# Four raw buffers for the input weights, their loads a chunk ahead, and an earlier start for converting the output weights, in an attention kernel with two feed-forward layers

## Chip, cores and metric

The kernel runs on one core of a Trainium2 chip. The metric is the device time of one execution in microseconds (us). Instructions go to five engines, each with its own in-order queue: TensorE (PE, matrix products), VectorE (DVE), ScalarE (ACT), GpSimd (POOL) and SyncE (SP). SP and ACT also issue the DMA transfers. A matmul has a weight load (PEld) beside it.

## What is computed

The first part is attention in two steps, over 8 batches of 8 heads, 576 positions, head size 64, with 32 packed queries p per head. Then two feed-forward layers follow on 4608 tokens, with d_model 512 and d_ff 2048:

```python
p_packed = sm_attn(p, k, v)                  # softmax(p k^T / 8) v
out = sm_attn(q, p_packed, p_packed)
x = out.transpose(0, 2, 1, 3).reshape(B * S, H * D)
h = x @ w_in;   x = (h * cos(h)) @ w_out     # first layer
h = x @ w_in2                                # second layer
g = where(h >= 1, h, where(h <= -1, 0, (h + 1)**2 / 4));  return g @ w_out2
```

Inputs are 64-bit floats.

## The kernel before

Weights arrive as 64-bit floats. A tile of 128 x 512 of them is loaded as pairs of 32-bit words (512 KB), and `convert` (L126 to L142) turns it into 32-bit floats: one ACT pass over the high words (L132) and five DVE passes (L134, L135, L138, L139, L142). `split` (L66 to L68) then writes a value as a high and a low part, one ACT copy (L67) and one subtraction on DVE or POOL (L68), so that three matmuls (`TERMS`) make a product of full precision.

The work is written as Python generators, one queue ("stream") each for loads, weights, attention, and so on. The main loop takes one step of each stream per item. A scheduler then orders the instructions of each engine by a timeline of its own, so that neighbours in the program may change places. The order is fixed when the kernel is built.

The stages are these:

1. Opening. `cut_w_in(c)` (L397) loads and converts the input weights `w_in` in 4 chunks of 4 tiles. Only two buffers `raw` hold loaded words: two loads are issued ahead, and each further load is issued once a tile has been converted. Beside it run the attention of the first batches (`stage1`, `stage2`) and `form_first`, which forms M = p_packed times `w_in` (matmuls at L426, moves of the parts by DMA at L447, split into `m` tiles). The tile pool `mpool` has 6 buffers of 8 KB for `m`.
2. Batches. 128 items `up(n, hf, fp)` (L604) run over 8 batches n, two halves hf and 8 pairs fp. An item is 12 matmuls into `hps` (L618), a copy to `u` (on ACT at L627, on DVE at L625 for every fourth item) and a store of `u` to DRAM (`h1T<-u`, issued by ACT at L86). `hps` has two banks. In the stream "wo" runs `cut_w_out` (L509): 16 tiles of `w_out` are loaded (L518, by SP, into two buffers that attention used before), converted and split into `wo`. The `wo` tiles take the buffers of the pool `wpool` that held the input weights `wi`, after their last matmul. The M of later batches is loaded by SP as `ml<-mB` (L498).
3. First down product, `run_down1` (L779). Tiles `h` are loaded from DRAM (L776, SP), ACT scales them (L792), DVE removes the whole turns (L793), ACT takes the sine (L800, after one table load), DVE multiplies (L801), `split` makes `r` (L67, L68), and the matmuls at L827 take `r` and `wo`. The tiles `h`, `t` and `r` lie in memory that the tiles of stages 1 and 2 had, and wait until those are free. Beside it `combine` converts and combines the second layer's weights (tiles `raw`, `pa`, `pl`, stores `su<-raw` and `su<-pl`).
4. `run_up2` and `run_down2`, which the change does not touch.

The line that starts the conversion of `w_out` is in the loop over items:

```python
if n == B - 3 and fp == 0 and hf == 1:
    streams["wo"].append(cut_w_out())
```

In the changed kernel, lines behind L393 have numbers higher by 7 to 9: L407 loads `w_in` there, L526 loads `w_out`, L626, L633 and L635 are the items' matmul and copies, L801, L802, L809, L810 are ACT's scaling, DVE's turns, the sine and DVE's product of `run_down1`.

Of the kernel before, what the change touches and what calls it, by code (L numbers as in the profile page):

```python
# [11 lines left out]
I32 = mybir.dt.int32  # L12
# [15 lines left out]
def body(ctx: ExitStack, tc: tile.TileContext, q, k, v, p, w_in, w_out, w_in2, w_out2, out):  # L28
    nc = tc.nc
    B, HP, _, S = q.shape  # L30
# [9 lines left out]
    NCH = DFF // 512  # L40
# [6 lines left out]
    mpool = ctx.enter_context(tc.tile_pool(name="mpool", bufs=6))  # L47
# [18 lines left out]
    def split(hi, lo, src, eng=None):  # L66
        nc.scalar.activation(out=hi, in_=src, func=AF.Copy)  # L67
        (eng or nc.gpsimd).tensor_tensor(out=lo, in0=src, in1=hi.bitcast(F32), op=ALU.subtract)  # L68
        return hi, lo
# [4 lines left out]
    def behind(last):  # L74
        return tc.issue_after(last[-1]) if last else nullcontext()
# [44 lines left out]
    def drain(*names):  # L120
        while any([step(name)[0] for name in names or streams]):
            pass

    def words(src):
        return src.bitcast(I32)

    def convert(raw, a, after=()):

        hi, lo = raw[..., 1], raw[..., 0]
        hf, lf = raw.bitcast(F32)[..., 1], raw.bitcast(F32)[..., 0]  # L130
        with behind(after):
            nc.scalar.activation(out=hf, in_=hf, func=AF.Copy, scale=2.0 ** -112)  # L132
        ai = a.bitcast(I32)
        nc.vector.tensor_scalar(out=ai, in0=hi, scalar1=3, scalar2=None, op0=ALU.logical_shift_left)  # L134
        nc.vector.scalar_tensor_tensor(  # L135
            out=ai, in0=hi, scalar=-(1 << 31), in1=ai, op0=ALU.bitwise_and, op1=ALU.bitwise_or
        )
        nc.vector.tensor_scalar(out=hi, in0=ai, scalar1=-(1 << 23), scalar2=None, op0=ALU.bitwise_and)  # L138
        nc.vector.scalar_tensor_tensor(  # L139
            out=lf, in0=lo.bitcast(U32), scalar=2.0 ** -52, in1=hf, op0=ALU.mult, op1=ALU.mult  # L140
        )
        nc.vector.tensor_tensor(out=a, in0=a, in1=lf, op=ALU.add)  # L142
# [11 lines left out]
    stg = ph2.enter_context(tc.tile_pool(name="stg", bufs=1, side="right"))  # L154
# [180 lines left out]
    def stage2(m, bufs=bufs_b):  # L335
        yield from until(("pt", m))
        if m:
            yield from until(("at", m - 1, 1))
        ts = [load_T(q, m, G, bufs, "q" if late else "qk") for G in range(2)]
        xs = att.tile([128, 4, NTB, 32], F32, tag="x", name="x")  # L340
        yield

        def evac(G, hf, ps):
            nc.vector.transpose(out=xs[:, 2 * hf + G], in_=ps[:, :HB].rearrange("p (a b) -> p a b", b=32))

        yield from scores(ts, bufs, lambda hp: PT[m][:, hp], evac)
        ready.add(("s2", m))
        x = xs.rearrange("p i a b -> p (i a) b")
        mx = wk.tile([128, 4 * NTB], F32, tag="mx2", name="mx2")
        nc.vector.tensor_reduce(out=mx, in_=x, axis=AX.X, op=ALU.max)  # L350
        nc.gpsimd.tensor_tensor(
            out=x, in0=x, in1=mx.unsqueeze(2).to_broadcast([128, 4 * NTB, 32]), op=ALU.subtract
        )
        yield
        with tc.high_priority(offset=PRI_EXP):
            nc.scalar.activation(out=xs, in_=xs, func=AF.Exp, scale=scale)
        yield
        sm = wk.tile([128, 4 * NTB], F32, tag="sm2", name="sm2")
        nc.vector.tensor_reduce(out=sm, in_=x, axis=AX.X, op=ALU.add)
        nc.vector.tensor_scalar(out=sm, in0=sm, scalar1=1e-9, scalar2=None, op0=ALU.add)  # L360
        nc.vector.reciprocal(out=sm, in_=sm)
        yield
        for hf in range(2):
            i = slice(2 * NTB * hf, 2 * NTB * hf + 2 * NTB)
            nc.gpsimd.tensor_tensor(
                out=x[:, i], in0=x[:, i], in1=sm[:, i].unsqueeze(2).to_broadcast([128, 2 * NTB, 32]), op=ALU.mult
            )
            X[m, hf] = x[:, i]
        yield
        ready.add(("x", m))  # L370

    def weights_T(m, hf):
        yield from until(("x", m))
        if m == 1:
            at = stg.tile([128, 2, 2, HB], F32R, tag="at1", name="at1", bufs=2)
        else:
            at = wk.tile([128, 2, 2, HB], F32R, tag="at", name="at")
        a32 = wk.tile([128, 2, HB], F32, tag="y2", name="a32", bufs=1)
        nc.vector.transpose(out=a32.rearrange("p g (a b) -> p (g a) b", b=32), in_=X[m, hf])
        yield  # L380
        split(at[:, :, 0], at[:, :, 1], a32)
        AT[m, hf] = at
        yield
        ready.add(("at", m, hf))
# [8 lines left out]

    WI = {}

    def cut_w_in(c):
        def load(hp):  # L397
            raw = stg.tile([128, 512, 2], I32, tag="raw", name="raw", bufs=2)
            src = words(w_in[hp * 128:(hp + 1) * 128, c * 512:(c + 1) * 512])
            nc.sync.dma_start(out=raw, in_=src.rearrange("p (c t) -> p c t", t=2))  # L400
            return raw

        raws = [load(hp) for hp in range(2)]
        for hp in range(4):
            if hp % 2 == 0:
                t = wpool.tile([128, 2, 2, 512], F32R, tag="w", name="wi")
            a = stg.tile([128, 512], F32, tag="w32", name="w32", bufs=2)  # L407
            convert(raws[hp], a)
            yield
            if hp < 2:  # L410
                raws.append(load(hp + 2))
            split(t[:, hp % 2, 0], t[:, hp % 2, 1], a, nc.vector)
            WI[c, hp] = t[:, hp % 2]
            ready.add(("wi", c, hp))
            yield
# [92 lines left out]
    def make_M(n, c):  # L508
        streams["load"].append(load_M(n, c))  # L509
# [121 lines left out]
    def spare(pool, tag, name, n):  # L631
        return [pool.tile([128, 2048], F32, tag=tag, name=f"{name}{i}") for i in range(n)]

    kv = spare(wpool, "w", "kv", 4)
    nk, nv = 2 * S, (KC + 1) * 4 * D  # L635
    pp1 = wk.tile([128, 2, 2, HB], F32, tag="at", name="pp1").rearrange("p a b c -> p (a b c)")[:, :HP * 128]
    bufs_0 = Bufs([(ps_a, "psA"), (ps_a, "psC")])
# [135 lines left out]
    def load_h1(i):  # L773
        if i < B * 16:
            t = dn1["g"].tile([128, 2, HB], F32, tag="g", name="h1")
            nc.sync.dma_start(out=t, in_=h1T[i % 8, :, i // 8])  # L776
            G1[i] = t
# [215 lines left out]
    for i, (n, hf, fp) in enumerate(items):  # L993
        if i == n_first // 2:
            streams["mat"].append(stage2(2))
            make_M(2, 0)
            make_M(2, 1)
        if i in (n_first - 4, n_first - 2):
            streams["load"].append(weights_T(2, (i - n_first) // 2 + 2))
        if i == 3 * n_first // 4:  # L1000
            make_M(2, 2)
            make_M(2, 3)
        if i == n_first + 1:
            drain("wt")
            ph2.close()
            late.append(ph2.enter_context(
                tc.tile_pool(name="late", bufs=1, reuse_waits="tile", side="right")))
        if n == B - 3 and fp == 0 and hf == 1:
            streams["wo"].append(cut_w_out())
        if i >= n_first and fp == 0 and hf == 0 and n + 1 < B:  # L1010
            streams["mat"].append(stage2(n + 1))
            make_M(n + 1, 0)
            make_M(n + 1, 1)
        if n == B - 1 and hf and fp == 0:
            drain()
            ph2.close()
            ph1.close()
            for x in ("y", 0, 1, "d"):
                up2[x] = pu.enter_context(
                    tc.tile_pool(name=f"up_{x}", bufs=1, reuse_waits="tile", side="right"))  # L1020
            dn1["g"] = pd.enter_context(tc.tile_pool(name="dn_g", bufs=8, reuse_waits="tile", side="right"))
            dn1["r"] = pd.enter_context(tc.tile_pool(name="dn_r", bufs=4, reuse_waits="tile", side="right"))
            for j in range(7):
                load_h1(j)
        up(n, hf, fp)
        if i >= n_first:
            if fp == 7 and n + 1 < B:
                streams["load"].append(weights_T(n + 1, hf))
            if hf and fp in (1, 3) and n + 1 < B:
                make_M(n + 1, fp // 2 + 2)  # L1030
        begin_stores(1)
        for name in ("load", "wt", "wo", "frm", "mat", "att", "load", "mat", "att", *(("att",) if i < n_first else ())):
            step(name)
# [54 lines left out]
```

## Time and profile before

| | us |
|---|---|
| three runs: median (lowest to highest) | 1709.02 (1708.21 to 1716.55) |
| the profiled execution | 1708.01 |
| its span, first to last instruction | 1706.0 |
| PE busy | 1566.5 |
| DVE busy | 1228.0 |
| ACT busy | 938.1 |

The profile is of one execution. Its own time lies 2.0 us above its span. The mean clock that TensorE was granted is 0.953 of its full 2.4 GHz; at its lower level of 1.2 GHz a stretch shows 0.50. A stage is best read by a table of windows: how long each engine was busy in a stretch of the span, and the clock in it.

### The profile page before, as it was taken

How to read it: one execution, taken by the hardware profiler on the slowest of the kernel's cores; microseconds unless marked ns; L12 is line 12 of the kernel's file. 1: busy time of each engine (PE TensorE's matmuls, PEld its weight loads, DVE VectorE, ACT ScalarE, POOL GpSimd, SP SyncE). 2: the span in 40 equal slices, each digit the busy share in tenths (PEclk: the TensorE clock that was granted, in tenths of full speed). 3: DMA queues.
4: the chain of work that ended last, by engine and by line, in shares of the span. 5: the costliest groups of instructions: out<-in, count | busy, mean ns of one | idle time of the engine just before them, and what ended most of it. 6: DMA issues, size and time to landing. Idle time of an engine off the chain costs nothing.

```text
span 1706.0 us, 28414 instructions
## 1 busy us (share of the span) xinstructions
PE 1566.5 (92%) x10846; PEld 1504.0 (88%) x10846; DVE 1228.0 (72%) x1787; ACT 938.1 (55%) x1530; POOL 231.9 (14%) x154
## 2 busy tenths in 40 slices
PE   9579988999819999999999989989999799999998
PEld 7459876998809999999998988889999799999998
DVE  6873434457869889987773889979766687777774
ACT  4443443445447667776663666766766444444443
POOL 1220101221100200000003224434331000000000
PEclk7779998999959999999999999999999899999999
DMA  7666797797667677664337455654437844444431
GB/s 258 161 194 215 226 298 242 234 298 255 239 200 220 194 268 245 212 204 131 113 91 272 153 184 207 212 208 167 174 133 308 339 151 131 128 132 139 139 105 36
DMA packets 177993, 333.23 MB, mean 195 GB/s; under 512 B 16576, under 2 KB 70848, under 8 KB 174272
## 3 DMA queue, kind: packets, MB, share of 16 engines
q1 hardware_dynamic: 123584, 237.02, 44.5%
q10 hardware_dynamic: 54272, 94.39, 14.8%
q8 instruction: 85, 1.39, 0.3%
q14 instruction: 52, 0.43, 0.1%
HBM read 190.84 MB, written 136.31 MB: 192 GB/s over the span
## 4 chain that ended last, share of the span: by engine, by line
PE 60%; DMA 16%; DVE 16%; issue 4%; ACT 3%; SPq 1%; ACTq 0%; DVEq 0%
PE psZ L932 9%; PE hps L618 8%; PE psZ L827 7%; PE psY L932 6%; PE psX L932 5%; PE psZ L747 5%; PE psX L747 3%; DMA raw<-in_moe_w_out 3%; PE psX L827 3%; PE psY L827 3%; PE psY L747 3%; DMA raw<-in_moe_w_in 3%; PE psA L279 2%; DVE t L733 2%; DVE raw L139 1%
## 5 line engine op out<-in xcount | busy, mean ns | idle before, releaser
L67 ACT ACTIVATE r<-g 128x576 fp32r<-128x576 f32 x224 | 153.4, 686 | 180.2 <-PE psZ L932 71.6
L618 PE MATMUL hps<-at,m 128*128 128x288 f32 x1536 | 234.8, 307 | 16.7 <-ACT u L627 8.2
L618 PEld LDWEIGHTS hps<-at,m 128*128 128x128 f32 x1536 | 216.4, 193 | 28.8 <-ACT u L627 10.7
L68 DVE TENSOR_TENSOR r<-g,r 128x576 fp32r<-128x576 f32 x224 | 166.7, 755 | 70.2 <-ACT r L67 70.1
L827 PE MATMUL psZ<-r,wo 128*128 128x288 f32 x1536 | 206.6, 296 | 0.9 <-DVE r L68 0.9
L827 PEld LDWEIGHTS psZ<-r,wo 128*128 128x128 f32 x1536 | 205.3, 188 | 1.4 <-DVE r L68 1.4
L827 PE MATMUL psX<-r,wo 128*128 128x288 f32 x768 | 125.9, 298 | 38.7 <-ACT r L67 35.8
L932 PE MATMUL psZ<-r,sw 128*128 128x288 f32 x1152 | 158.2, 296 | 1.6 <-DVE o L725 0.9
L932 PEld LDWEIGHTS psZ<-r,sw 128*128 128x128 f32 x1152 | 155.0, 188 | 2.0 <-issue 1.1
L827 PEld LDWEIGHTS psX<-r,wo 128*128 128x128 f32 x768 | 110.6, 190 | 40.2 <-ACT r L67 36.0
L733 DVE SCALAR_TENSOR_TENSOR t<-hh,t 128x576 f32<-128x576 f32 x128 | 119.0, 937 | 34.5 <-ACT t L732 33.3
L731 ACT ACTIVATE t<-hh,half 128x576 f32<-128x576 f32 x128 | 97.8, 771 | 61.5 <-DVE hh L725 45.3
L68 DVE TENSOR_TENSOR r<-t,r 128x576 fp32r<-128x576 f32 x128 | 99.3, 776 | 39.5 <-ACT r L67 39.4
L747 PE MATMUL psZ<-ty,sw 128*128 128x288 f32 x768 | 114.5, 299 | 14.2 <-DVE hh L725 14.2
L68 POOL TENSOR_TENSOR ty<-td,ty 128x576 fp32r<-128x576 f32 x32 | 55.1, 1726 | 522.6 <-DMA yT<-o 320.4
L827 PE MATMUL psY<-r,wo 128*128 128x288 f32 x768 | 124.1, 297 | 0.0
L747 PEld LDWEIGHTS psZ<-ty,sw 128*128 128x128 f32 x768 | 106.1, 190 | 16.8 <-DVE hh L725 16.8
L67 ACT ACTIVATE r<-t 128x576 fp32r<-128x576 f32 x128 | 87.1, 680 | 51.5 <-PE psY L827 26.7
L932 PE MATMUL psX<-r,sm 128*128 128x288 f32 x768 | 107.5, 300 | 8.5 <-ACT r L67 8.3
L932 PEld LDWEIGHTS psX<-r,sm 128*128 128x128 f32 x768 | 105.3, 192 | 9.1 <-ACT r L67 8.6
L827 PEld LDWEIGHTS psY<-r,wo 128*128 128x128 f32 x768 | 110.2, 189 | 0.0
L800 ACT ACTIVATE t<-t,halfpi 128x576 f32<-128x576 f32 x128 | 97.9, 768 | 19.9 <-DVE t L793 19.7
(164 smaller groups left out, 2833.6 us busy)
## 6 DMA issues: line engine op xcount, KB each, us to landing
h1T<-u ACTq DMA_DIRECT2D x128, 288.0 KB, 3.3
h<-h1T SPq DMA_DIRECT2D x128, 288.0 KB, 3.4
gT<-t ACTq DMA_DIRECT2D x128, 288.0 KB, 2.7
g<-gT SPq DMA_DIRECT2D x128, 288.0 KB, 3.2
raw<-in_moe_w_in SPq DMA_DIRECT2D x32, 512.0 KB, 5.6
raw<-in_moe_w_out SPq DMA_DIRECT2D x32, 512.0 KB, 4.9
mB<-cp SPq DMA_DIRECT2D x96, 128.0 KB, 3.6
ml<-mB SPq DMA_DIRECT2D x48, 256.0 KB, 4.5
```

Of the source, the lines that this page charges most:

```text
L67: nc.scalar.activation(out=hi, in_=src, func=AF.Copy)
L68: (eng or nc.gpsimd).tensor_tensor(out=lo, in0=src, in1=hi.bitcast(F32), op=ALU.subtract)
L139: nc.vector.scalar_tensor_tensor(out=lf, in0=lo.bitcast(U32), scalar=2.0 ** -52, in1=hf, op0=ALU.mult, op1=ALU.mult)
L279: nc.tensor.matmul(out=pp[:, s * 64:s * 64 + 64], lhsT=ve[:, s * 128:s * 128 + 128], rhs=e[:, pos * 64:pos * 64 + 64], start=(c == 0), sto ...
L618: nc.tensor.matmul(out=hps[:, j, :HB], lhsT=m[:, w, G, cs], rhs=x[:, G, y], start=(G == 0 and i == 0), stop=(G == 1 and i == 2),)
L731: nc.scalar.activation(out=t, in_=h, func=AF.Relu, scale=0.5, bias=half)
L733: nc.vector.scalar_tensor_tensor(out=t, in0=h, scalar=1.0, in1=t, op0=ALU.max, op1=ALU.min)
L747: nc.tensor.matmul(out=ps[:, i], lhsT=s[:, d, w, cs], rhs=t[:, d, y], start=first and d == n == 0, stop=d == 1 and n == 2, skip_group_chec ...
L800: nc.scalar.activation(out=t, in_=t, func=AF.Sin, scale=2 * PI, bias=halfpi)
L827: mm = nc.tensor.matmul(out=acc[d // 2][:, d % 2], lhsT=wo[f // 4, w][:, f % 4, ds], rhs=r[:, y, k], start=f == n == 0, stop=f == NFT - 1 ...
L932: nc.tensor.matmul(out=ps[:, j], lhsT=s[:, f % 4, w, j * 128:j * 128 + 128], rhs=r[:, y, k], start=first and f == n == 0, stop=f == 7 and ...
```

## The change

The opening gets four buffers for loaded words instead of two. The third and fourth (`raw2`) are made from one 8 KB tile of `mpool`, which M uses later. All four tiles of chunk 0 are loaded at the start, and each conversion of chunk c is followed at once by the load of the same tile of chunk c + 1. And `cut_w_out` is put into its stream one batch (16 items) sooner.

```diff
     def cut_w_in(c):
-        def load(hp):
-            raw = stg.tile([128, 512, 2], I32, tag="raw", name="raw", bufs=2)
+        def load(c, hp):
+            i = n_raw[0] % 4
+            n_raw[0] += 1
+            if i < 2:
+                raw = stg.tile([128, 512, 2], I32, tag="raw", name="raw", bufs=2)
+            else:
+                raw = raw2[:, i - 2].rearrange("p (c t) -> p c t", t=2)
...
-        raws = [load(hp) for hp in range(2)]
+        if c == 0:
+            ahead[0] = [load(0, hp) for hp in range(4)]
         for hp in range(4):
...
-            convert(raws[hp], a)
+            convert(ahead[c][hp], a)
+            if c + 1 < NCH:
+                ahead.setdefault(c + 1, []).append(load(c + 1, hp))
             yield
-            if hp < 2:
-                raws.append(load(hp + 2))
             split(t[:, hp % 2, 0], t[:, hp % 2, 1], a, nc.vector)
...
+    raw2 = spare(mpool, "m", "raw", 1)[0].bitcast(I32).rearrange("p (a b) -> p a b", b=1024)
...
-        if n == B - 3 and fp == 0 and hf == 1:
+        if n == B - 4 and fp == 0 and hf == 1:
             streams["wo"].append(cut_w_out())
```

On SP, at the start of the program, the queue before issues two loads of `w_in` words and then the values v of attention:

```order
L400 DMA raw<-in_moe_w_in 128x1024 x2
L221 DMA vraw<-in_v 128x4x256
L224 DMA vraw<-in_v 64x256
L221 DMA kv_122<-in_v 128x4x256
L224 DMA kv_122<-in_v 64x256
L195 DMA qk<-in_q 128x2x576 x2
L309 DMA pp<-in_p 128x512
L400 DMA raw<-in_moe_w_in 128x1024
```

The same place in the changed kernel (`raw_124` is the tile `raw2`):

```order
L407 DMA raw<-in_moe_w_in 128x1024 x2
L407 DMA raw_124<-in_moe_w_in 128x1024 x2
L221 DMA vraw<-in_v 128x4x256
L224 DMA vraw<-in_v 64x256
L221 DMA kv_122<-in_v 128x4x256
L224 DMA kv_122<-in_v 64x256
L195 DMA qk<-in_q 128x2x576 x2
L309 DMA pp<-in_p 128x512
L407 DMA raw<-in_moe_w_in 128x1024
```

Two loads have moved ahead of all loads of v and q.

On DVE, at the end of the items, the queue before starts with the last copy of an item (L625) and goes on with the conversion of `w_out` (the tiles `w_4187`, `w_4230` and `w_4273` are three of its last four; the last one and a piece of `combine` follow):

```order
L625 COPY u<-hps 128x576
L134 TENSOR_SCALAR w_4230<-raw 128x512
L68 TENSOR_TENSOR wo<-w_4187,wo 128x512
L135 SCALAR_TENSOR_TENSOR w_4230<-raw,w_4230 128x512
L138 TENSOR_SCALAR raw<-w_4230 128x512
L139 SCALAR_TENSOR_TENSOR raw<-raw 128x512
L134 TENSOR_SCALAR w_4273<-raw 128x512
L142 TENSOR_TENSOR w_4230<-w_4230,raw 128x512
L135 SCALAR_TENSOR_TENSOR w_4273<-raw,w_4273 128x512
L138 TENSOR_SCALAR raw<-w_4273 128x512
L68 TENSOR_TENSOR wo<-w_4230,wo 128x512
```

In the changed kernel DVE's queue has, up to and behind the last copy of an item (L633; `w_4023` is the last tile of `w_out`):

```order
L68 TENSOR_TENSOR wo<-w_3968,wo 128x512
L138 TENSOR_SCALAR raw<-w_4023 128x512
L633 COPY u<-hps 128x576
L139 SCALAR_TENSOR_TENSOR raw<-raw 128x512
L142 TENSOR_TENSOR w_4023<-w_4023,raw 128x512
L68 TENSOR_TENSOR wo<-w_4023,wo 128x512
L633 COPY u<-hps 128x576
L802 SCALAR_TENSOR_TENSOR t<-h_4354,t 128x576
L802 SCALAR_TENSOR_TENSOR t<-h_4356,t 128x576
```

Four of the 16 splits into `wo` stand behind the last copy before, and none after. Counted in items on DVE and ACT, the splits stand at items 92 to 128 before and at 77 to 125 after.

On ACT, at the start of `run_down1`, the queue before ends the last `wo` and the first unit of `combine` before it begins (the names in brackets are what a row waits for: DMAHW0 to DMAHW7 are DMA transfers):

```order
L67 ACTIVATE wo<-w_4316 128x512 [waits DVE_49]
L67 ACTIVATE raw<-raw 128x512 [waits DMAHW2_49,DMAHW3_49,DVE_49,Activation_49]
L67 ACTIVATE pl<-raw 128x512 [waits DMAHW4_49,DVE_49,Activation_49]
L792 ACTIVATE t<-h_4361 128x576 [waits DMAHW5_49,Pool_49]
L792 ACTIVATE t<-h_4363 128x576 [waits DMAHW6_49]
L800 ACT_TABLE_LOAD
```

In the changed kernel it begins with the last stores of the items:

```order
L635 ACTIVATE u<-hps 128x576 [waits DMAHW3_49,DMAHW0_49,PE_49]
L86 DMA h1T<-u 128x576 [waits Activation_49]
L86 DMA h1T<-u 128x576 [waits DMAHW4_49,DVE_49]
L801 ACTIVATE t<-h_4354 128x576 [waits DMAHW6_49,Pool_49]
L801 ACTIVATE t<-h_4356 128x576 [waits DMAHW7_49,DMAHW4_49,DMAHW0_49]
L801 ACTIVATE t<-h_4358 128x576 [waits DMAHW1_49]
L801 ACTIVATE t<-h_4360 128x576 [waits DMAHW2_49]
L809 ACT_TABLE_LOAD
L809 ACTIVATE t<-t,halfpi 128x576 [waits DVE_49] x4
L67 ACTIVATE r_4525<-t 128x576 [waits DVE_49]
```

The piece of `combine` has moved behind the first `r`, and the second scaling waits for two more transfers than before.

## Rows read from the trace of the kernel before

**Rows 1.** The page: busy time of each engine, share of the span, instructions.

```profile
PE 1566.5 (92%) x10846; PEld 1504.0 (88%) x10846; DVE 1228.0 (72%) x1787; ACT 938.1 (55%) x1530; POOL 231.9 (14%) x154
```

**Rows 2.** Windows: stretch, its length, busy time and instructions by engine, clock, DMA.

```profile
12.00:118.30 106.30, 74.93 (x280) 55.63 (x279) 92.01 (x166) 49.90 (x104) 22.30 (x13) 0.70 0.67 193
20.00:40.00 20.00, 19.38 (x73) 16.15 (x74) 15.12 (x33) 8.84 (x26) 2.14 (x2) 0.50 0.61 190
363.00:395.00 32.00, 31.98 (x228) 30.91 (x227) 18.29 (x25) 15.88 (x26) 9.11 (x6) 1.00 0.78 276
395.00:474.80 79.80, 67.93 (x475) 63.94 (x473) 67.45 (x110) 41.95 (x70) 9.44 (x6) 1.00 0.74 248
474.80:510.60 35.80, 0.05 (x1) 0.05 (x1) 23.68 (x39) 13.49 (x21) 0.00 (x0) 0.53 0.59 193
510.60:770.00 259.40, 255.61 (x1891) 253.89 (x1892) 233.72 (x346) 185.11 (x291) 8.74 (x5) 0.99 0.69 224
```

**Rows 3.** Timeline around the stretch 474.8 to 510.6: start, us, engine, line, operation, tiles, count.

```profile
471.12 3.63 PE L618 MATMUL hps<-at,m 128*128 128x288 f32 x24 [2.17 <-ACT u L627]
...
498.35 0.68 DVE L68 TENSOR_TENSOR wo<-w,wo 128x512 fp32r<-128x512 f32 x1
...
499.63 4.51 SPq L776 DMA_DIRECT2D h<-h1T  x8
...
506.05 1.28 ACT L800 ACT_TABLE_LOAD   x1
...
510.55 0.61 PE L827 MATMUL psX<-r,wo 128*128 128x288 f32 x1 [35.80 <-ACT r L67]
```

**Rows 4.** Tile t, 495 to 530 us: ns min/median/max, first and last start.

```profile
L792 ACT ACTIVATE t<-h x12: 667/668/687, 504.6 to 528.0; 128x576 int32<-128x576 f32 x12
...
L800 ACT ACTIVATE t<-t,halfpi x11: 759/763/777, 507.3 to 529.7; 128x576 f32<-128x576 f32 x11
...
L67 ACT ACTIVATE r<-t x9: 668/672/692, 509.8 to 529.1; 128x576 fp32r<-128x576 f32 x9
```

**Rows 5.** The page, DMA issues: count, KB each, median us to landing.

```profile
h1T<-u ACTq DMA_DIRECT2D x128, 288.0 KB, 3.3
```

**Rows 6.** DVE by line, 363 to 475 us: busy, mean ns, idle before.

```profile
L625 DVE COPY u<-hps 128x576 f32<-128x576 f32 x15 | 11.3, 752 | 8.5 <-PE hps L618 6.8 <-DMA h1T<-u 1.3 <-issue 0.4
```

**Rows 7.** Waits of DVE, 12 to 126 us.

```profile
DVE w L134 <- ACT raw L132: 9.6, 8, 1.9
```

**Rows 8.** Tile raw, 0 to 130 us: first ACT pass, and time from issue to landing.

```profile
L132 ACT ACTIVATE raw<-raw x16: 651/676/698, 11.8 to 106.4; 128x512 f32<-128x512 f32 x16
...
DMA to landing us min/median/max: 3.8/5.1/8.7
```

**Rows 9.** Timeline of the opening: first load and first use of v.

```profile
4.89 0.44 SPq L221 DMA_DIRECT2D vraw<-in_v  x1
...
15.57 1.00 PE L279 MATMUL psA<-e,vraw 128*128 128x64 f32 x8
```

**Rows 10.** Windows of the opening, and tile vraw: time from issue to landing.

```profile
6.00:8.00 2.00, 2.00 (x10) 1.58 (x9) 0.00 (x0) 0.47 (x2) 0.00 (x0) 1.00 1.05 407
...
DMA to landing us min/median/max: 4.4/5.7/9.9
```

**Rows 11.** PE by line, 395 to 474.8 us.

```profile
L618 PE MATMUL hps<-at,m 128*128 128x288 f32 x463 | 66.0, 300 | 11.8 <-ACT u L627 7.4 <-DVE u L625 4.3
```

**Rows 12.** Tile wo, 280 to 520 us: the ACT half of its splits.

```profile
L67 ACT ACTIVATE wo<-w x16: 612/630/636, 401.4 to 496.8; 128x512 fp32r<-128x512 f32 x16
```

**Rows 13.** Timelines of DVE and of POOL, 415.5 to 420 us.

```profile
416.61 2.62 DVE L68 TENSOR_TENSOR wo<-w,wo 128x512 fp32r<-128x512 f32 x1
...
416.24 2.45 POOL L351 TENSOR_TENSOR x<-x,mx 128x1152 f32<-128x1152 f32 x1 [5.56 <-DVE mx L350]
```

**Rows 14.** Waits of SP's queue, 395 to 474.8 us.

```profile
SPq L518 <- DVE w L142: 41.4, 11, 8.1
```

**Rows 15.** Windows of tile pa (the first unit of combine) alone.

```profile
474.80:510.60 35.80, 6.26 (x10) 0.94 (x2) 0.53 0.59 193
```

More of the change, by code (lines that the diff above doesn't have):

```diff
@@ L394, in body @@
     WI = {}
+    n_raw, ahead = [0], {}
     def cut_w_in(c):
-        def load(hp):
-            raw = stg.tile([128, 512, 2], I32, tag="raw", name="raw", bufs=2)
+        def load(c, hp):
[5 more added lines that the diff above has]
+                raw = raw2[:, i - 2].rearrange("p (c t) -> p c t", t=2)
             src = words(w_in[hp * 128:(hp + 1) * 128, c * 512:(c + 1) * 512])
```

## The prediction

> **What bounds the kernel now.** I read the page first: PE is busy 92% of the span and no other engine comes near [rows 1]. So time is to be had only where PE stands still or runs at its lower clock, and the next view is a table of windows by stage [rows 2]. It shows two places that the edits touch. In the opening, 12 to 118.3 us, PE is busy for 74.9 of 106.3 us at a clock of 0.70, and DVE for 92.0: DVE sets the pace there. From 474.8 to 510.6 us PE has one matmul in 35.8 us. Ahead of that gap, among the last items, it loses some 12 of 79.8 us; behind 510.6 it is full, 255.6 of 259.4 us.
>
> The timeline around that gap comes next, with what ended each wait [rows 3]. The first matmul of the down product waits 35.8 us for ACT's first `r`, and the rows ahead say why. The last item's matmuls end at 471.12 + 3.63 = 474.75. The last piece of `wo` leaves DVE at 498.35 + 0.68 = 499.0. At 499.63 SP begins the loads of `h`, whose memory was in use until then, and at 510.55 PE starts. So 24.9 us of the gap pass until the loads, and 10.9 us are the restart proper. The 16 pieces of `wo` come at a pace of (496.8 - 401.4) / 15 = 6.4 us [rows 12]; the first comes too late for the last to be ready with the items' end.
>
> **The gap.** The change starts the conversion a batch sooner. On DVE no split into `wo` stands behind the last copy of an item any more. I therefore take the 24.9 us out and work out a new restart from the order on ACT: the last copy of an item, 0.75 [rows 6]; its store, which the second scaling waits for (its memory was that of a `u`), 3.3 to landing [rows 5]; three more scalings at 0.67 (2.0), the table load 1.28 [rows 3], four sines at 0.76 (3.05) and the first copy into `r`, 0.67 [rows 4]. That is 11.05 us, so the gap shrinks by 35.8 - 11.05 = 24.8. If the wait is for an older store, the 4.05 fall to one copy and one scaling more, 0.75 + 0.67: the gap is 8.4 and the gain 27.4. If `wo` ends late and `h` is loaded only after the last copy, the 10.9 of today's restart come behind a rest of one tile, 6.4 by its pace: 17.3, and a gain of 18.5. The order speaks for the middle value.
>
> The Trainium skill (ScalarE: Activation LUTs, What ACT_TABLE_LOAD costs) adds a drain to a table switch and gives some 2.66 us in all. The row shows 1.28. By the page the new gap would be 1.4 us longer.
>
> What the gap covered has to run elsewhere: the first unit of `combine`, 6.26 us of DVE on its tile `pa` alone [rows 15]. It moves under the first down product, where DVE is idle for 259.4 - 233.7 = 25.7 us up to 770 [rows 2]. Hidden it costs 0; without cover 6.3 and some smaller passes, 9 at most (estimate: half as much again). I take 1.5, nearer to hidden, since DVE at 90% sometimes delays an `r`.
>
> **The batches.** The conversion itself is not less work. The order has the splits at items 77 to 125, so about 15 items earlier; at 32.0 us / 228 = 0.14 us a matmul [rows 2] and 12 an item that is 25 us, to a start near 376 and, at 6.4 us a piece, an end near 472, just ahead of the last item. From 395 to 474.8 PE now loses 11.8 us to late copies of `u` on ACT and DVE [rows 11], queued behind conversion work. Two things change: about four more tiles fall among the items (4 / 12 of 11.8 is 4 us more), and they are spread, (125 - 77) / 15 = 3.2 items a tile where the order before had (128 - 92) / 15 = 2.4, so that copies wait less (a quarter, 3 us less). I take 0, with bounds of -8 (most of the wait goes) and +8 (twice that for the four more tiles).
>
> Moved forward, the tiles also meet more work of POOL: 9.1 us of it in the 32 from 363 to 395, against 9.4 in the 79.8 behind [rows 2]. The trace shows what that does: one subtraction of DVE takes 2.62 us beside a POOL pass of 2.45, where the next to the gap takes 0.68 [rows 13, 3]. Prorated, 9.1 - 9.4 x 32 / 79.8 = 5.3 us of DVE time more. If it all delays the last `wo`, it eats 5.3 of the 24.8.
>
> The Trainium skill (SBUF — State Buffer, Who interferes with whom) says that a DVE instruction with two SBUF inputs and a GpSimd one that reads SBUF block each other fully, the later waiting for the earlier's end. It speaks against this change, which puts DVE's passes beside more of POOL's; the trace agrees in the pair above.
>
> **The opening.** DVE's work stays: 16 tiles by five passes and a split. What goes are waits: 9.6 us in 8 of them in which DVE waits for ACT's first pass [rows 7], which itself comes when a load has landed, 5.1 us after its issue in the median, 8.7 at most [rows 8]. The 16 first passes stand at 11.8 to 106.4 us, so 6.3 apart [rows 8]. With a load issued when its buffer's conversion ends and three tiles converted in between, a load has about 19 us for its 8.7: covered. I take 9 of the 9.6. The most is DVE's whole idle time, 106.3 - 92.0 = 14.3 [rows 2]; the least is 0, if SP's queue, in which the loads wait for their buffers, holds back the moves of M instead and DVE then waits for those.
>
> Against it stands that two loads more, 1.05 MB, go ahead of v and q. At 407 GB/s [rows 10] they delay these by 2.6 us. v is issued at 4.89 and used at 15.57 [rows 9], and lands 5.7 later in the median, 9.9 at most [rows 10]: 4.89 + 5.7 + 2.6 = 13.2 is in time, with 9.9 it is 17.4, 1.8 late. I take 0 and keep 1.8. M's buffers: one fewer while `raw2` lives, but the first M is used up four items in, and its buffer then serves; cost 0, and if it isn't, one or two items, 1.7 to 3.4.
>
> **Sum.** -9 (opening) - 24.8 (gap) + 1.5 (`combine`) + 0 (batches) = -32.3. The profiled execution took 1708.0 us (span 1706.0), 0.06% below the median of the runs shown. 1708.0 - 32.3 = 1675.7; I predict 1676.
>
> **The rivals.**
> - The opening gives nothing: DVE's idle time moves from waits on words to waits on M's parts, which SP queues behind the loads of words. For it: from 20 to 40 us PE is busy for 19.4 of 20 us at the lower clock [rows 2], so there a faster conversion feeds nobody. Against: the 8 waits are in DVE's own queue. 1708.0 - 24.8 + 1.5 + 1.8 = 1686.5.
> - The gap is not emptied: the tiles keep their pace or slow down by POOL's 5.3 us, and `wo` ends behind the last copy. For it: 472 is close to 474.8. Then the gap gains 18.5, and the batches lose up to 8: 1708.0 - 9 - 18.5 + 1.5 + 8 = 1690.
> - Slower: SP's queue. Loads of words wait there for DVE, 41.4 us in 11 waits, 8.1 at most [rows 14], and in the changed order ten of the 16 have loads of M for the last two batches behind them. M is asked for a batch ahead, 16 items or 27 us, which absorbs as much. At the mean, 3.8, ten waits are 38: 11 us late, still faster by 21. It decides from (27 + 32) / 10 = 5.9 us a wait; at 8.1 the end is 1708.0 - 32 + 81 - 27 = 1730. Against it: the waits can overlap with M's lead more than once.
> - The change doesn't do what it says: the starting batch moves nothing, because `wo` needs buffers of `wi`. Against: in the order the splits have moved by 15 items. About 1700 (opening only).
>
> **How the numbers follow.** Forecast: 0.68, by itself 1663 to 1688 (opening 14 to 4, gap 27.4 to 20, batches -5 to +2). Opening without gain: 0.13. Gap not emptied: 0.11. No effect of the start: 0.04. Slower: 0.02. Better than the forecast's range: 0.02. The range 1661 to 1692 leaves out the last three and a rest of the others, some 12 in 100. A measurement can tell about 0.5%, or 8.5 us, from no change. Faster by more: the first three and the best, 0.94, less a rest: 0.93. Within 0.5%: 0.05, slower: 0.02.
>
> **What the profile after would show.** Right: DVE waits for ACT's first pass of `w_in` words nearly gone, last input tile converted near 109 us instead of 118; the gap ahead of the first L836 matmul 8 to 13 us and behind it no `wo` left; PE's idle time among the items near 12 us; DVE nearer to full from 470 to 700. Wrong: a gap above 17 us, waits of the items' matmuls for `m` in the last batches, or a stretch to the end of the opening that is as long as before, with DVE or PE waiting for L455's moves.

## The result, and the profile after

The changed kernel takes 1679.91 us (median of 4 runs, 1676.02 to 1687.23) against 1709.67 for the kernel before on the same chip: a ratio of 0.985, 95% interval 0.982 to 0.987. On a second chip it was 1681.03 us (6 runs) against 1706.11, ratio 0.9856 [0.9833, 0.988]. The change is 25 to 30 us faster; 1676 was forecast, in a range of 1661 to 1692.

The profiled execution is the slowest of the first four (1687.23 us, span 1685.2), so its parts sum to 20.8 us and not to 30. Its page (busy time of each engine, to be set beside [rows 1]):

```profile
PE 1566.7 (93%) x10846; PEld 1506.5 (89%) x10846; DVE 1225.1 (73%) x1787; ACT 937.1 (56%) x1530; POOL 229.1 (14%) x154
```

The windows of the kernel after, columns as in [rows 2]; the third row is the new gap:

```profile
12.00:118.30 106.30, 74.46 (x293) 56.29 (x292) 93.14 (x166) 52.07 (x109) 19.47 (x14) 0.70 0.68 198
20.00:40.00 20.00, 19.30 (x98) 16.55 (x98) 18.95 (x40) 11.82 (x33) 3.19 (x4) 0.74 0.86 273
472.70:485.10 12.40, 0.08 (x2) 0.04 (x1) 6.24 (x9) 7.24 (x11) 0.00 (x0) 0.59 0.91 309
485.10:770.00 284.90, 277.87 (x2040) 276.37 (x2041) 252.12 (x375) 198.97 (x312) 8.82 (x5) 0.98 0.68 217
```

The gap is 12.4 us where it was 35.8. In the opening DVE is not less busy over the whole stretch, but in 20 to 40 us it is busy for 18.95 us instead of 15.12, and PE's granted clock there is 0.74 instead of 0.50. The down product, in contrast, is less full than it was: 7.0 us idle in 284.9, against 3.8 in 259.4.

The timeline around the new gap answers to [rows 3]:

```profile
469.73 0.69 DVE L68 TENSOR_TENSOR wo<-w,wo 128x512 fp32r<-128x512 f32 x1 [1.22 <-ACT wo L67]
473.03 0.76 DVE L633 COPY u<-hps 128x576 f32<-128x576 f32 x1 [2.61 <-DMA h1T<-u]
474.25 0.68 ACT L801 ACTIVATE t<-h 128x576 int32<-128x576 f32 x1 [2.41 <-DVE u L633]
478.52 1.83 ACT L801 ACTIVATE t<-h 128x576 int32<-128x576 f32 x3 [3.58 <-DMA h1T<-u]
480.36 1.28 ACT L809 ACT_TABLE_LOAD   x1
481.66 2.77 ACT L809 ACTIVATE t<-t,halfpi 128x576 f32<-128x576 f32 x4
484.34 1.24 ACT L67 ACTIVATE r<-t 128x576 fp32r<-128x576 f32 x2
485.06 0.61 PE L836 MATMUL psX<-r,wo 128*128 128x288 f32 x1 [12.32 <-ACT r L67]
```

The last split into `wo` ends at 470.4, ahead of the items' last matmul. What is left is the restart on ACT that the prediction added up: the last copy, the wait for a store of `u` (ACT stands idle for 3.58 us), three scalings, the table load, four sines, the first `r`. Tile `wo`, to be set beside [rows 12]:

```profile
L67 ACT ACTIVATE wo<-w x16: 615/628/641, 369.9 to 469.1; 128x512 fp32r<-128x512 f32 x16
```

The waits of PE from 465 to 900 us (what waited for what: us in total, times, longest) have the gap, and behind it 6.2 us for DVE's splits into `r`:

```profile
PE psX L836 <- ACT r L67: 12.3, 1, 12.3
PE psX L836 <- DVE r L68: 3.1, 2, 2.6
PE psZ L836 <- DVE r L68: 3.1, 2, 1.7
```

DVE's waits in the opening, to be set beside [rows 7]: the 9.6 us for ACT's first pass have become 1.0, and a wait for a product of `form_first` has grown from 7.0 (first row, of the kernel before) to 9.8.

```profile
DVE cp L430 <- PE psD L426: 7.0, 2, 6.6
```

```profile
DVE cp L438 <- PE psD L434: 9.8, 2, 7.9
DVE w L134 <- ACT raw L132: 1.0, 1, 1.0
```

### The profile page after: what moved, and what is told of

The parts are those of the page before. It is cut to its first block, busy times and chain, and to the rows that moved or that the text cites. A ratio compares the mean times of both kernels' runs of the same rounds, so it can differ in the third digit from the quotient of the medians.

```text
span 1685.2 us, 28435 instructions
## 1 busy us (share of the span) xinstructions
PE 1566.7 (93%) x10846; PEld 1506.5 (89%) x10846; DVE 1225.1 (73%) x1787; ACT 937.1 (56%) x1530; POOL 229.1 (14%) x154
## 4 chain that ended last, share of the span: by engine, by line
PE 52%; DVE 22%; DMA 17%; issue 5%; ACT 3%; SPq 1%; ACTq 0%; DVEq 0%
PE psZ L941 9%; PE hps L626 7%; PE psY L941 6%; PE psZ L836 5%; PE psX L941 5%; PE psZ L756 4%; DMA raw<-in_moe_w_in 3%; PE psY L756 3%; PE psX L756 2%; PE psY L836 2%; PE psX L836 2%; DVE t L742 2%; DVE r L68 2%; DVE t L802 2%; DVE raw L139 2%
## 5 line engine op out<-in xcount | busy, mean ns | idle before, releaser
L626 PE MATMUL hps<-at,m 128*128 128x288 f32 x1536 | 239.6, 311 | 16.7 <-ACT u L635 7.5
L626 PEld LDWEIGHTS hps<-at,m 128*128 128x128 f32 x1536 | 221.7, 197 | 28.9 <-ACT u L635 10.3
L836 PE MATMUL psX<-r,wo 128*128 128x288 f32 x768 | 126.0, 299 | 15.5 <-ACT r L67 12.3
L756 PE MATMUL psZ<-ty,sw 128*128 128x288 f32 x768 | 115.2, 300 | 15.0 <-DVE hh L734 15.0
L836 PEld LDWEIGHTS psX<-r,wo 128*128 128x128 f32 x768 | 111.2, 190 | 16.6 <-ACT r L67 12.6
```

The source lines that it names most:

```text
L626: nc.tensor.matmul(out=hps[:, j, :HB], lhsT=m[:, w, G, cs], rhs=x[:, G, y], start=(G == 0 and i == 0), stop=(G == 1 and i == 2),)
L756: nc.tensor.matmul(out=ps[:, i], lhsT=s[:, d, w, cs], rhs=t[:, d, y], start=first and d == n == 0, stop=d == 1 and n == 2, skip_group_chec ...
L836: mm = nc.tensor.matmul(out=acc[d // 2][:, d % 2], lhsT=wo[f // 4, w][:, f % 4, ds], rhs=r[:, y, k], start=f == n == 0, stop=f == NFT - 1 ...
```

## Stages, from one profile of each kernel

For this table the trace was read for the start of the last split of an input tile, the start of the last matmul of the items, the gap (start of that matmul to the start of the down product's first), and the lengths of the down product and of `run_up2` (first matmul to the next stage's first). "Late yb" is the edit of the second group of experiments.

| kernel | last input tile | items end | gap | down product | up2 | span | off the median |
|---|---|---|---|---|---|---|---|
| before | 117.6 | 474.5 | 36.1 | 417.0 | 398.9 | 1706.0 | -1.0 |
| start alone | 120.6 | 475.1 | 12.9 | 425.2 | 400.3 | 1692.9 | +1.0 |
| buffers alone | 115.1 | 474.2 | 33.3 | 426.2 | 402.6 | 1715.7 | +6.3 |
| after | 112.9 | 472.4 | 12.6 | 422.6 | 398.4 | 1685.2 | +7.3 |
| after, second profile | 111.2 | 465.5 | 11.9 | 418.6 | 397.9 | 1674.7 | -4.3 |
| after, words by POOL's queue | 110.5 | 469.4 | 12.5 | 420.8 | 401.0 | 1683.4 | +6.2 |
| before, late yb | 118.1 | 476.5 | 35.0 | 420.1 | 396.9 | 1708.4 | +3.8 |
| start alone, late yb | 121.0 | 478.1 | 12.6 | 417.2 | 402.0 | 1690.0 | +6.6 |
| buffers alone, late yb | 112.6 | 463.7 | 36.5 | 418.1 | 401.3 | 1699.8 | -4.8 |
| after, late yb | 112.0 | 464.6 | 12.3 | 416.1 | 398.2 | 1670.9 | -2.2 |
| after, late yb, t elsewhere | 111.5 | 467.8 | 7.6 | 416.0 | 395.3 | 1666.8 | -5.7 |
| after, late yb, start half a batch later | 109.9 | 471.8 | 11.4 | 418.9 | 396.4 | 1678.1 | -6.1 |
| after, late yb, start half a batch sooner | 115.2 | 477.9 | 12.1 | 418.2 | 402.9 | 1690.3 | +7.8 |
| after, late yb, without the low words | 66.9 | 457.1 | 13.2 | 417.4 | 398.1 | 1666.3 | -8.2 |

Each row is one execution, and the last column says how far its time lies from the median of its kernel's runs: differences between rows of a few us can be those of the executions and not of the kernels.

## Experiments: the parts apart

**The changed kernel again**, for a second profile.

> The changed kernel itself once more, for a second profile beside the parts of it. Theory: the gap ahead of the down product is again about 12 us (12.3 in the first profile), the end of the items again only some 2 to 3 us earlier than before, and the ratio again about 0.985. In the first profile the down product itself took 5.6 us more than before (stalls at 550 to 570 and 630 to 650 us, granted clock 0.91 there). If that is the price of the moved combine, the second profile has it too; if it is one execution's bad luck, it is absent and the span is some 5 us shorter.

1681.03 us, ratio 0.9856 [0.9833, 0.988]. The gap repeats (11.9). The items end 7 us sooner than in the first profile, and the down product takes 418.6 us: so the first profile's 422.6 was mostly one execution's. Of its two stalls the later one repeats (PE waits of 0.79 and 1.66 us in the first profile, 0.74 and 1.66 in the second), the earlier one does not. These are two rows of it from the first profile, and the first of the two as the second profile has it (`yb` is the first input of `run_up2`, loaded ahead):

```profile
553.04 0.69 ACT L67 ACTIVATE ty<-yb 128x576 fp32r<-128x576 f32 x1 [5.27 <-DMA yb<-yT]
...
563.45 1.46 PE L836 MATMUL psX<-r,wo 128*128 128x288 f32 x5 [2.65 <-DVE r L68]
```

```profile
542.97 0.69 ACT L67 ACTIVATE ty<-yb 128x576 fp32r<-128x576 f32 x1 [2.62 <-DMA yb<-yT]
```

ACT waited 2.65 us longer for the load of `yb`, and 10 us later PE waited 2.65 us for `r`; in the second profile no wait of PE there is over 0.5.

**The start alone.**

```diff
-        if n == B - 3 and fp == 0 and hf == 1:
+        if n == B - 4 and fp == 0 and hf == 1:
```

> The kernel before with only the start of the output weights' conversion one batch sooner (B - 4). Theory (the gap is the whole of the gain, the opening gives about 2 to 3): gap 35.8 to about 12, opening as before (last input tile near 118 us), ratio about 0.987, some 22 us faster than before. Rival (the opening gives the 9 us that were forecast and something else eats them): this kernel would keep the whole of the gap's gain, without what eats it, or lack 9 us of the change's gain: ratio 0.990 or more.

1693.98 us, ratio 0.9929 [0.9903, 0.9954]: 12 us faster, about half of the theory's 22 and on the rival's side of 0.990. But what ate the gain is in this kernel too, without the buffers: the gap did shrink to 12.9, and the down product grew by 8 us, to 425.2.

**The buffers alone**: the changed kernel with `n == B - 3`.

> The changed kernel with the start of the output weights' conversion put back to B - 3: four raw buffers and loads a chunk ahead alone. Theory: the gap stays at about 36 us, DVE's waits for the first pass of the input words fall from 9.6 to about 1 us, the last input tile is some 3 us earlier, and the kernel gains 1 to 3 us (ratio 0.998 to 1.000). Rival, the forecast's term: 9 us, ratio 0.9947. A second rival: nothing at all, or slower by up to 1.8 us through the later loads of v and q.

1711.19 us, ratio 1.0022 [1.0004, 1.0041]: 5 us slower, more than any of the three had. The down product again, 426.2 us, although here the gap is still there (the profile is the slowest of the twelve runs). So the parts gain 12.1 and -5.1 us, 7 in sum, and together 25.1. By the table most of the missing 18 lies in the down product and in up2, stages whose code is the same in all four kernels; some 6 us of it are the items' end, which came sooner with both edits than with either.

**The input words by POOL's queue.**

```diff
-            nc.sync.dma_start(out=raw, in_=src.rearrange("p (c t) -> p c t", t=2))
+            (nc.gpsimd if c else nc.sync).dma_start(out=raw, in_=src.rearrange("p (c t) -> p c t", t=2))
```

> The changed kernel with the loads of the input words from the second chunk on issued from POOL's queue instead of SP's, so that no load of q or move of M stands behind a load of words that waits for its buffer. Theory (the opening's 9 us were lost in SP's queue: PE waits 5.4 us at 47.8 us for a load of q that was issued behind two loads of words, and SP's moves of M wait 46 us in all where they waited 25 before): that wait of PE goes, and the opening ends up to 6 us sooner than in the changed kernel, ratio about 0.981. Rival (the opening is bound by DVE's work and by PE at its lower clock, whatever the queue): the last input tile stays near 112 us and the ratio near 0.985; POOL's splits then wait behind the loads and it may be slower by a few us.

1679.25 us, ratio 0.9854 [0.9831, 0.9877], the same as the change. Here are the waits of PE in the first 130 us, of the changed kernel and then of this one:

```profile
PE psC L434 <- ACT wi L67: 9.0, 2, 7.3
PE psA L207 <- DMA qk<-in_q: 5.4, 1, 5.4
...
PE psA L279 <- DMA vraw<-in_v: 1.7, 1, 1.7
```

```profile
PE psC L434 <- ACT wi L67: 8.7, 2, 7.9
PE psD L434 <- ACT wi L67: 6.5, 3, 3.7
```

The wait for q is gone, others have grown, the last input tile comes at 110.5. SP's queue cost nothing that counts. The wait for v stands in the first profile of the change alone; the second has none.

## Experiments: where the down product lost

In the profile of the start alone, this stands in the timeline of the down product (some rows of POOL, DVE and PE):

```profile
561.02 2.08 POOL L698 TENSOR_TENSOR td<-yb 128x576 f32<-128x576 f32 x1 [110.78 <-DMA yb<-yT]
...
561.72 1.99 DVE L793 SCALAR_TENSOR_TENSOR t<-h,t 128x576 f32<-128x576 f32 x1
...
563.06 1.93 POOL L68 TENSOR_TENSOR ty<-yb,ty 128x576 fp32r<-128x576 f32 x1
...
563.64 1.97 DVE L68 TENSOR_TENSOR r<-t,r 128x576 fp32r<-128x576 f32 x1
...
565.53 1.92 DVE L138 TENSOR_SCALAR raw<-pa 128x1024 int32<-128x1024 int32 x1
...
568.03 2.44 DVE L139 SCALAR_TENSOR_TENSOR raw<-raw 128x1024 f32<-128x1024 uint32 x1
...
569.46 2.26 POOL L698 TENSOR_TENSOR td<-yb,td 128x576 f32<-128x576 f32 x1
570.39 1.95 DVE L68 TENSOR_TENSOR r<-t,r 128x576 fp32r<-128x576 f32 x1
572.26 0.75 DVE L793 SCALAR_TENSOR_TENSOR t<-h,t 128x576 f32<-128x576 f32 x1
...
572.39 1.81 PE L827 MATMUL psZ<-r,wo 128*128 128x288 f32 x6 [3.26 <-DVE r L68]
```

`yb` is loaded as soon as its tokens are stored, some 60 us into the down product. POOL then has five passes on it. While they last, a DVE pass of 576 elements takes 1.95 to 1.99 us instead of 0.75, and splits into `r` come late: PE waits for 1.41 us and then for 3.26. Behind the second wait its clock is at the lower level for some time:

```profile
572.40:577.90 5.50, 5.50 (x23) 5.50 (x24) 5.50 (x10) 4.71 (x8) 0.00 (x0) 0.50 0.10 14
```

At the 0.14 us a matmul of [rows 2] these 23 would take 3.2 us, so the clock costs 2.3 more (an estimate from the two rows). In the kernel before, the passes (577.3 to 586.9 us) are followed by one wait of 0.85 at 587.6, and a further one of 0.94 comes 14 us behind. The Trainium skill (SBUF — State Buffer, Who interferes with whom) has DVE instructions with two SBUF inputs and GpSimd ones that read SBUF exclude each other; the rows agree, 1.97 us beside POOL's 1.93.

So all four kernels were run with this load held back in SP's queue to step 104 of 128, where no `combine` runs any more:

```diff
-            nc.sync.dma_start(out=t, in_=h1T[i % 8, :, i // 8])
+            last_h[:] = [nc.sync.dma_start(out=t, in_=h1T[i % 8, :, i // 8]).ins]
...
-                first_y = load_y(0)
-                next(first_y)
+                with tc.issue_after(last_h[0]):
+                    first_y = load_y(0)
+                    next(first_y)
```

> The kernel before, with the first load of yb in the down product held in SP's queue behind the h load of step 104, some 280 us later, past the combine of the first product's weights. Theory: what made the two parts of the change not add up is one place in the down product, where ACT waits for yb to land and POOL's five passes stretch DVE's from 0.75 to 1.98 us; in the kernel before it cost only some 2 us of PE (0.85 + 0.94 of waits), so here 1 to 3 us are gained, ratio 0.998 to 0.9995. Rival (the place is not what costs): no change.

1706.37 us, ratio 1.0004 [0.9987, 1.0021]: no change, the rival's result. The wait of 0.85 is gone, but two of 2.33 and 1.66 us stand at 632 and 634 us, where no pass on `yb` is near, and the down product of this profile is 3 us longer (420.1).

> The earlier start alone, with the same late load of yb. Theory: its down product, 425.2 us in the run without this edit, falls to about 415, the gap stays at 12 to 13, and the kernel comes to about 1684 us, ratio 0.986 to 0.988 (without the edit 0.9929). Rival (the 8 us that the start alone gives back in the down product are the combine that the gap covered before, not the place of yb): the down product stays at 422 or more, ratio 0.992.

1685.53 us, ratio 0.9868 [0.9841, 0.9895]; down product 417.2. As the theory had it: some 8.5 us came back, and the down product is 8.0 shorter.

> The four raw buffers alone, with the same late load of yb. Theory: the down product, 426.2 us in the run without this edit although the gap was there, falls to about 416, and what is left is the opening's small gain: about 1702 us, ratio 0.996 to 0.999 (without the edit 1.0022). Rival: no change, ratio 1.002.

1706.34 us, ratio 1.0008 [0.999, 1.0027]; down product 418.1. 5 of the 9 us forecast came back, and nothing is left as the buffers' own gain; the profile, second fastest of twelve, is 4.8 us better than that.

> The changed kernel with the same late load of yb. Theory: down product from 418.6 and 422.6 us in the two profiles to about 415, time about 1677 us, ratio 0.982 to 0.984; and the gains of the two parts over the kernel before with a late yb then add up to that of both, within 3 us. Rival (the place is not what costs, the parts do not add for another reason): ratio 0.9855 as before, and the sum of the parts' gains stays 10 us or more short of the gain of both.

1674.89 us, ratio 0.9821 [0.9803, 0.984]; down product 416.1. These are the waits of PE from 460 to 905 us; of the 6.2 us that it waited for DVE's `r` in the first profile of the change, 1.1 are left:

```profile
PE psX L836 <- ACT r L67: 12.0, 1, 12.0
PE psX L756 <- ACT p L729: 2.9, 1, 2.9
PE psZ L836 <- ACT r L67: 1.4, 1, 1.4
PE psZ L836 <- DVE r L68: 1.1, 1, 1.1
```

The parts now gain 20.8 and 0.0 us, 20.9 in sum, together 31.5: 10.6 short, where 18.0 were short (the intervals of the four ratios are 3 to 5 us to either side). The forecast of 3 failed. By the table, what both edits gain beyond the sum of the parts is, in the down product, 13.8 us without the late load (425.2 + 426.2 - 417.0 - 420.6, the last the mean of two profiles) and -0.9 with it (417.2 + 418.1 - 420.1 - 416.1): that place was the larger part, although 3 of this change are the other waits in the kernel before with a late yb. In up2 it is 5.9 and 8.2 (402.0 + 401.3 - 396.9 - 398.2), which the edit does not touch. There the waits of PE are, for the start alone and then for the kernel before, both with a late yb:

```profile
PE psZ L747 <- DVE hh L725: 15.3, 9, 3.5
PE psX L747 <- ACT p L720: 8.2, 4, 4.6
PE psY L747 <- DVE hh L725: 7.3, 5, 3.1
```

```profile
PE psZ L747 <- DVE hh L725: 14.2, 12, 2.8
PE psX L747 <- ACT p L720: 10.3, 4, 4.7
PE psY L747 <- DVE hh L725: 1.2, 2, 0.6
```

The order of the program is laid out anew whenever anything in it moves. In up2 the traces show two orders and not four: PE and DVE have the same sequence in the kernel before and in the changed one, with or without the late load (396.9 to 398.9 us), and the two parts share another, but for a few places (400.3 to 402.6). So either edit alone tips the order, and both together tip it back. Not all of the difference is waits: with a late yb PE idles for 31.9 us in up2 with the start alone and for 26.2 in the kernel before, both at a granted clock of 0.98; with the buffers alone it idles for 27.0, and there the clock is 0.96. Two more kernels bound the price: the changed kernel with its words by POOL's queue has the first order and took 401.0, the one without the low words has the second and took 398.1. Which rows of the order make the difference was not tried.

## Experiments: the gap, the start and the opening

All four start from the changed kernel with a late yb (1674.89 us, ratio 0.9821). They ran on another chip, on which the kernel before takes 1704.21 us, so the ratios are the fairer comparison.

**`t` elsewhere.**

```diff
-        po = pd.enter_context(tc.tile_pool(name="dn_o", bufs=3, reuse_waits="tile"))
-        pt = pd.enter_context(tc.tile_pool(name="dn_t", bufs=4, reuse_waits="tile"))
...
         prep[:] = [pd.enter_context(tc.tile_pool(name="prep1", bufs=1, reuse_waits="tile"))]
+        po = pd.enter_context(tc.tile_pool(name="dn_o", bufs=3, reuse_waits="tile"))
+        pt = pd.enter_context(tc.tile_pool(name="dn_t", bufs=4, reuse_waits="tile"))
```

> The changed kernel with the late load of yb (1674.9 us), and the pool of the prepared weights opened ahead of those of o and t, so that no t of the first scalings lies where a u was. Theory: 3.3 to 3.6 us of the 12.3 us gap are the second scaling's wait for the store of the last u (as the prediction's sum had it: copy 0.75 + landing 3.3); without it the gap is 8.4 to 9 us and the kernel 3 to 4 us faster, about 1671.5. Rival: another wait of the same length stands behind it (an h load, the accumulators' memory), the gap stays at 12 and the time at 1675; or the places in memory make other waits and it is slower.

1674.23 us, ratio 0.9823 [0.98, 0.9846]. The timeline of the restart:

```profile
468.45 0.76 DVE L633 COPY u<-hps 128x576 f32<-128x576 f32 x1 [2.62 <-DMA h1T<-u]
469.61 1.25 ACT L801 ACTIVATE t<-h 128x576 int32<-128x576 f32 x2 [2.37 <-DVE u L633]
...
470.88 1.28 ACT L809 ACT_TABLE_LOAD   x1
...
475.39 0.61 PE L836 MATMUL psX<-r,wo 128*128 128x288 f32 x1 [7.26 <-ACT r L67]
```

The second scaling follows the first at once, and the gap is 7.3 us: the wait for the store (3.40 us with a late yb, 3.58 in the first profile) was real and could be taken out. The rest of the 4.7 us is the order on ACT, which has two sines instead of four ahead of the first `r`. The runs show no gain: the ratios are 0.9823 and 0.9821, with intervals of some 4 us to either side. The two spans (1666.8 and 1670.9) do differ by 4.1 us, but that is 4.7 less in the gap, 3.2 more ahead of it and 2.9 less in up2, where this kernel has an order of its own.

**Half a batch later and sooner** (`n == B - 3 and hf == 0`; `n == B - 4 and hf == 0`).

> The changed kernel with the late load of yb, and the output weights begun half a batch (8 items, some 14 us) later than the change has it, halfway between before and after. In the order the last two tiles of wo then stand level with the last copies of u. Theory: the gap follows the end of wo, which comes up to 7 us behind the items, and is 16 to 20 us; time 1679 to 1684. Rival (the conversion keeps its pace of 6.4 us a tile from its start, so wo ends 14 us later): gap about 26 us, time about 1689. Third: the tiles come faster when they begin later, and nothing is lost, gap 12, 1675.

1686.0 us, ratio 0.9882 [0.9859, 0.9904]. The gap is 11.4, the third theory's, although `wo` ends 3 us behind the items: the tiles come at (474.1 - 382.5) / 15 = 6.1 us, the loads of `h` begin at 474.1, and the rest of the restart hides the last tile. The time is nevertheless some 10 us longer, beyond the 1684 of the theory.

> The changed kernel with the late load of yb, and the output weights begun half a batch sooner still. Theory: the gap is at its floor, the restart of 12.3 us, which no earlier start shortens; time within 3 us of 1675. Rival: the start is still short, the gap falls below 11 us and the time to 1672 or less. Third rival: the earlier tiles meet more of POOL's passes and delay the copies of u among the items, 3 us or more slower.

1684.34 us, ratio 0.9881 [0.9862, 0.9901]. The gap is 12.1, its floor, as the theory had it; the tiles slow down to 7.1 us each. The time is some 10 us longer, not within 3: the third rival's side. Its mechanism shows in part: PE's waits among the items are 19.2 us against 15.8, and those for copies of `u` 15.1 against 11.6. The profile is the slowest of the six runs, 19.4 us longer than that of the kernel it started from. Of these, 13.3 are the items' end, with the opening at the low clock (below), and 4.8 are up2, which has the parts' order here. For the half batch later the profile is one of the two fastest of six runs, and what its median lost is not settled. Neither loss is in the gap.

**Without the low words**: the conversion of `w_in` leaves out the low word's share (L139 and L142).

> The changed kernel with the late load of yb; left out is the low word's share in the conversion of the input weights of the first product, two of DVE's five passes, 26.1 us of DVE in the 16 tiles of the opening (L139 and L142 in the profile). Theory (what is left of the opening is set by DVE's own work, not by a queue): the last input tile comes 20 to 26 us sooner, near 90 us, and the items end some 15 to 20 us sooner; time about 1657. Rival (PE at its lower clock, or SP's moves of M, sets the pace as soon as the waits for the words are gone): less than 8 us sooner, time 1668 or more.

1676.39 us, ratio 0.9825 [0.9801, 0.9848]: no gain, the rival's. The window of 12 to 118.3 us, then tile `wi`, then the longest of DVE's waits:

```profile
12.00:118.30 106.30, 83.77 (x355) 64.81 (x353) 72.16 (x139) 56.93 (x118) 19.09 (x14) 0.74 0.70 215
```

```profile
L68 DVE TENSOR_TENSOR wi<-w,wi x16: 642/682/951, 14.9 to 66.9; 128x512 fp32r<-128x512 f32 x16
```

```profile
DVE e L267 <- PE psA L260: 12.6, 2, 11.8
```

With 21 us less of DVE's work the last input tile is ready 45 us sooner, at 66.9, but the first item starts at 74.1, no sooner than in the other kernels (69 to 74), and DVE waits for PE. Its one profile does have the items end at 457.1; it is the fastest of six runs, and the median has nothing of it.

## Why the prediction was right where it was, and where not

**The gap** (-24.8): right, in size and in mechanism. Measured -23.5 and -24.2 by the table (36.1 to 12.6 and 11.9). The sum of 11.05 us had the order and, but for one, the lengths. From the end of the items' last matmul (472.7) to the second scaling (478.52) it had 4.05 us, a copy and 3.3 for the store, chosen over the bound of 8.4 without that wait; 5.8 passed. The rest, to 485.06, took 6.5 for 7.0. The table load was 1.28 us again, with the first sine 0.02 behind it: the 1.4 us more that the prediction set beside its sum did not come there, although 11.05 + 1.4 lies near the 12.3 measured.

**The opening** (-9): mis-sized, and what it is worth is not settled. The waits went as forecast, 9.6 to 1.0 us, the loads were covered, and PE waited 1.7 us for v in the first profile, which the prediction had put at 0 with 1.8 as the risk. But the last input tile came at 112.5 us, mean of the eight profiles with four buffers and this order, for 119.3 in the four with two: 6.8 us sooner, not 9; and the items' end moved from 476.1 to 469.8, 6.3 us. In the changed kernel's own two profiles it moved by 2.0 and 8.9. The medians of the runs agree on no size: the buffers alone gain nothing (-5.1 us, and 0.0 with a late yb), and beside the earlier start, with a late yb, 10.6. The statement that DVE sets the pace of the opening failed: the run without the low words shows that less work of DVE gives no shorter time. What goes with the rest is PE's clock. These windows of 20 to 40 us are those of the changed kernel with a late yb, of the same with an earlier start, and of the start alone; the first two have the same order of instructions to past 330 us:

```profile
20.00:40.00 20.00, 16.75 (x90) 15.05 (x89) 17.63 (x40) 9.74 (x27) 1.90 (x2) 0.76 0.83 270
```

```profile
20.00:40.00 20.00, 20.00 (x82) 17.79 (x81) 18.12 (x41) 9.74 (x26) 1.85 (x2) 0.50 0.76 244
```

```profile
20.00:40.00 20.00, 19.12 (x79) 16.45 (x80) 16.62 (x37) 9.45 (x27) 1.67 (x2) 0.54 0.64 200
```

With two buffers all four profiles have 0.50 to 0.54 there. With four buffers two of eight have 0.50 or 0.51: their first item starts at 72.9 and 73.3 us and their items end at 474.2 and 477.9, as without the buffers (72.3 to 74.0, and 474.5 to 478.1). The six at 0.59 to 0.76 start the items at 69.2 to 70.7 and end them at 463.7 to 472.4. So in these profiles the buffers gain where the clock is granted sooner, and nothing where it is not. That the clock is the cause is not shown: no run sets it, and among the six the two at 0.59 end at 465.5 and 467.8, the three at 0.74 anywhere from 463.7 to 472.4. The prediction had the reason among its rivals, with 0.13: where PE is busy at the lower clock, a faster conversion feeds nobody.

**`combine`** (+1.5): the size was short, and the cause incomplete. The down product took 1.5 and 5.6 us more than before. PE did wait for late splits into `r`, as the prediction said, but what made them late was not the unit's DVE time alone: it was where the load of `yb`, ACT's wait for it and POOL's passes fell among the splits. With that load late the same `combine` costs nothing, 416.1 us against 417.0 and 420.1. The prediction read only one unit of `combine` and never asked what POOL does behind the gap, though [rows 2] had its 8.74 us there.

**The batches** (0): right. Between the first and the last matmul the items took 402.0 and 395.8 us against 402.2, and PE waited among them 16.7 and 15.2 us for 16.7 (the group of the items' matmuls in the lines view).

**The rivals.** SP's queue made nothing slower, and taking the words out of it made nothing faster. The gap was emptied. Of the 32.3 us forecast, 29.8 and 25.1 came, 2.5 and 7.2 too few. By the profiles the opening fell short by 2.7, the gap by 1 and the down product by 2 (a mean of 3.6 for 1.5), 5.8 in all. That the sum came so close is in part luck: the opening's share stood on a wrong statement and varies by more than its error from one execution to the next.

The fastest versions are the changed kernel with the late load of yb (1674.89 us, 0.9821) and the same with `t` elsewhere (1674.23 us, 0.9823).

## What to carry to other kernels

A stall with one chain behind it can be priced well by adding that chain up from its rows, the landing of the last store included. A change that a scheduler lays out anew alters stages that it does not touch: the same two edits gave 12 and -5 us apart and 25 together, so read every stage of each variant before a gain is put down to an edit. Where DVE is over 90% busy, look for what POOL does beside it, and for loads whose landing an in-order engine waits for; moving one such load was worth 6 us.

## What the runs showed of the hardware that was not expected

The same order of instructions at the start of a program met a granted clock of 0.50 in one execution and 0.76 in another over 20 to 40 us, and 0.51 and 0.74 in a second pair; the items ended at 477.9 and 464.6, and at 474.2 and 463.7. It is not the chip: the kernels with `t` elsewhere, with the start half a batch later and with it half a batch sooner ran on one chip, with one order in the opening, and had 0.59, 0.74 and 0.50. A wait of PE of 3.26 us in a full stretch was followed by 5.5 us at 0.50, which cost about 2.3 more. The same two waits with the same order, 0.8 or 0.7 and then 1.66 us, were followed by a lower clock in one profile of the change (0.91 over 627 to 647 us) and by none in the other (1.00 over 617 to 637 us).
